# Mixture of experts on one core: three buffers for the groups' mixed rows, group rows turned ahead of the second layer, turned hidden rows apart from their use

## The chip, the cores and the metric

The kernel runs on one NeuronCore of a Trainium2 chip. A core has five engines that run side by side, each through its own instructions in order: TensorE (PE, matrix multiplies; PEld is its weight load), VectorE (DVE), ScalarE (ACT), GpSimd (POOL) and SyncE (SP, which here issues transfers). An instruction starts when the one before it on its engine has started its work and when the semaphores that it waits for have been raised by other engines or by transfers (DMA). The metric is device time in microseconds (us) of one execution; less is better.

## The reference

Two parts follow each other. The first is clustered attention over 4 batches, 8 heads and 768 positions, and its output gives 3072 rows x of 512 numbers. The second is a mixture of 8 experts, and this change is in the second alone:

```python
do_compute = x @ w_skip > 0
xc = x[do_compute]
logits = xc @ w_gate
e_idx = np.argmax(logits, axis=1)
gate_w = softmax(logits)[rows, e_idx]
for e in range(8):
    mask = e_idx == e
    h = np.maximum(xc[mask] @ w1[e], 0.0)      # 512 -> 1024
    y[mask] = gate_w[mask, None] * (h @ w2[e]) # 1024 -> 512
out[do_compute] = xc + y
```

## The kernel before

The attention's last matmuls with its values (L718) end soon after 421 us; the experts' work begins beside that and runs to the end of the kernel. One expert comes first (p = 0), and the others follow in the order of how many rows they have, p = 1 (most) to 7, and the table `SHAPE` says how each is cut: experts 1 and 2 have two tiles of 128 rows, experts 3 to 7 have one, and beside its tiles an expert has groups of 32 rows: expert 2 has group 0, expert 3 has groups 1 and 2, experts 4, 5 and 6 have groups 3, 4 and 5. Rows are fetched by an indirect DMA from GpSimd (`gather`, L1321, tiles `xg` for the 128-row tiles and slices of `PT` for groups) and written back by one (`scatter`, L1328).

**Tiles of 128 rows.** Each product is made of three matmuls of a high and a low half (`three`: L1139, L1140, L1141 in the second layer; L1158, L1161, L1162 in the first layer of a one-tile expert). ScalarE makes the high half of each weight (L1552), VectorE the low half (L1553). Hidden rows are made 512 at a time (`hidden_rows`, and ScalarE's Relu at L1164 into `PT`), and are turned with the rows on the free side by four PE transposes (`turn`, L1149), of which ScalarE copies the high half (L1151) and VectorE makes the low half (L1152). `turn(0)` is for the first four blocks f = 0 to 3 of the second layer, `turn(1)` for f = 4 to 7. `prepare(p + 1)` turns the next expert's rows in the same way (L1149 from `xg`, then L1151 and L1152).

**Groups of 32 rows.** A group's row is spread over four partitions, so that 32 rows fill a tile of 128 by 128. Its way is: `group_turn` (a transpose at L1627 and ScalarE's copy `oxt` at L1629), `group_hidden` (the first layer with plain float32 weights, L1636, and the Relu `ohs` at L1640), `group_back` (two transposes, L1646, and the copy `oht` at L1648) and, when that expert's turn has come, `group_result` (the second layer, L1655; then VectorE's `mix` at L1178 of the product, gate and row into the tile `oyo`, which is scattered). The tile `oyo` has one buffer. For expert p + 1 the first three steps are done in the middle of expert p's second layer, so that they lie beside it.

The order on each engine is set by the order of the code and by a scheduler that moves instructions where their inputs are expected later; semaphores do the rest. Weights come by SyncE's queue into a ring of eight buffers `wraw`, each freed when the matmuls and splits that read it are done.

Of the kernel before, what the change touches and what calls it, by code (L numbers as in the profile page):

```python
# [13 lines left out]
F32 = mybir.dt.float32  # L14
# [9 lines left out]
P = 128  # L24
# [13 lines left out]
E, DM, FF = 8, H * D, 1024  # L38
KD, KF = DM // P, FF // P
# [3 lines left out]
OC = P // OT  # L43
# [50 lines left out]
SHAPE = {1: (2, ()), 2: (2, (0,)), 3: (1, (1, 2)), 4: (1, (3,)), 5: (1, (4,)), 6: (1, (5,)), 7: (1, ())}  # L94


class Kernel:
# [1227 lines left out]
    def scatter(self, rows, ix, apart=True, parts=1):  # L1325

        dst = self.out if parts == 1 else self.out.rearrange("n (c d) -> (n c) d", c=parts)
        put = self.nc.gpsimd.indirect_dma_start(  # L1328
            out=dst, out_offset=bass.IndirectOffsetOnAxis(ap=ix, axis=0), in_=rows, in_offset=None,
            bounds_check=self.ntok * parts - 1, oob_is_err=False)  # L1330
        if apart:
            self.tc.declare_no_dep(put.ins, group="rows", reason="a token is in one slot: rows of two scatters differ")
            self.tc.add_to_no_dep_group("rows", put.ins)
# [190 lines left out]
    def experts(self, ctx):  # L1524
        tc, nc = self.tc, self.nc
        pool = lambda name, bufs, **k: ctx.enter_context(tc.tile_pool(name=name, bufs=bufs, **k))
        xp, hp, ot = pool("xp", 2), pool("hp", 1), pool("ot", 1)
# [6 lines left out]
        def psum(tag, *dims):  # L1534
            q = turns[tag]
            q.rotate(-1)
            t = q[-1][:, :int(np.prod(dims))]
            return t.rearrange("p (a b) -> p a b", a=dims[0]) if len(dims) > 1 else t
# [7 lines left out]
        def split(w, tag, pieces=1, part=slice(None)):  # L1546

            hi, lo = W[f"{tag}h"], W[f"{tag}l"]
            n = 1024 // pieces
            todo = [(slice(c * n, (c + 1) * n), *t) for c in range(pieces) for t in zip(w, hi, lo)]  # L1550
            for cs, r, h, l in todo[part]:
                nc.scalar.activation(out=h[:, cs], in_=r[:, cs], func=AF.Copy)  # L1552
                nc.vector.tensor_tensor(out=l[:, cs], in0=r[:, cs], in1=h.bitcast(F32)[:, cs], op=ALU.subtract)  # L1553
            return hi, lo
# [4 lines left out]
        def prepare(p):  # L1559

            x, n = rows(p), SHAPE[p][0]
            hi, lo = self.X1 if n == 1 else (xp.tile([P, KD, n * P], F32R, name=f"x{n}{c}", bufs=1) for c in "hl")
            self.turned([x[:, j, k * P:(k + 1) * P] for k in range(KD) for j in range(n)], hi, lo, bank)
            return hi, lo
# [60 lines left out]
        def group_turn(x):  # L1625
            tp = psum("tp", P)
            nc.tensor.transpose(out=tp, in_=x, identity=self.ident)  # L1627
            xt = ot.tile([P, KD, OT], F32, name="oxt", bufs=2)
            nc.scalar.activation(out=xt.rearrange("p k t -> p (k t)"), in_=tp, func=AF.Copy)  # L1629
            return xt  # L1630

        def group_hidden(xt, w1):
            ph = psum("ph", FF // OC)
            for k in range(KD):
                for c in range(OC):
                    nc.tensor.matmul(ph[c * OT:(c + 1) * OT, :], lhsT=xt[:, k, :],  # L1636
                                     rhs=w1[k][:, c * FF // OC:(c + 1) * FF // OC],
                                     start=(k == 0), stop=(k == KD - 1), skip_group_check=True)
            hs = ot.tile([P, KF // OC, P], F32, name="ohs", bufs=2)
            nc.scalar.activation(out=hs.rearrange("p m f -> p (m f)"), in_=ph, func=AF.Relu)  # L1640
            return hs

        def group_back(hs):
            th = psum("ph", KF // OC, P)
            for m in range(KF // OC):
                nc.tensor.transpose(out=th[:, m, :], in_=hs[:, m, :], identity=self.ident)  # L1646
            ht = ot.tile([P, KF // OC, OC, OT], F32, name="oht2", bufs=2)
            nc.scalar.activation(out=ht.rearrange("p m c t -> p m (c t)"), in_=th, func=AF.Copy)  # L1648
            return ht

        def group_result(ht, w2, x, oid, og, apart=True):
            py = psum("py", DM // OC)
            for f in range(KF):
                for c in range(OC):
                    nc.tensor.matmul(py[c * OT:(c + 1) * OT, :], lhsT=ht[:, f % (KF // OC), f // (KF // OC), :],  # L1655
                                     rhs=w2[f // 2][:, f % 2 * DM + c * DM // OC:f % 2 * DM + (c + 1) * DM // OC],
                                     start=(f == 0), stop=(f == KF - 1), skip_group_check=True)
            yo = ot.tile([P, DM // OC], F32, name="oyo")
            self.mix(yo, py, x, og)
            scatter(yo, oid, apart, parts=OC)  # L1660

        def rows(p):
            if xg[p % 3] is None:
                xg[0] = xp.tile([P, CT, DM], F32, name="xg0", bufs=1)
            return xg[p % 3]

        def gathers(p):
            for j in range(SHAPE[p][0]):
                gather(rows(p)[:, j, :], self.slots[0][p][:, j:j + 1])
# [5 lines left out]
        def group_first(p):  # L1675

            for g in SHAPE[p][1]:
                backs[g] = group_back(group_hidden(group_turn(self.XG[g]), self.halves[p, 0]))

        def ahead(n):  # L1680
            self.load_pieces(4 * n + RING - 12, 4 * n + RING - 8)


        backs = {}
        gathers(1)
        scatter(self.YE, self.early[0])
        gates = self.slot_gates(self.acc.rearrange("p v h e -> p v (h e)"), ot, P, CT * E, "")
# [2 lines left out]
        py = psum("py", DM)  # L1690
# [7 lines left out]
        xs = prepare(1)  # L1698
# [7 lines left out]
        for p in range(1, E):  # L1706
            tiles, mine = SHAPE[p]
            for g in mine:
                group_result(backs[g], self.halves[p, 1], self.XG[g], *groups[g][1:])
            if tiles == CT:  # L1710
                h = hidden(*xs, *w1s)
            else:
                hidden_rows(0)
                self.turn(0, bank)
                hidden_rows(1)
            if p == 1:
                mark = self.newest()
            w2s = split(self.halves[p, 1], "w2")
            ahead(2 * p + 4)
            if p + 2 < E:  # L1720
                gathers(p + 2)
            if p == 1:
                n0 = self.written()
                self.codes()
                for c in range(OC):
                    nc.vector.memset(self.cblock[c * OT:(c + 1) * OT, :], float(c))
                nc.vector.tensor_copy(self.again.rearrange("p (c t) -> p c t", c=OC),
                                      self.ident[:OT, :OT].unsqueeze(1).to_broadcast([OT, OC, OT]))
                far = ot.tile([P, 1], F32, name="far")
                nc.vector.tensor_scalar(out=far, in0=self.number[:, :1], scalar1=float(self.NG), scalar2=CAP // OT + 1.0,  # L1730
                                        op0=ALU.mult, op1=ALU.add)
                groups = {0: group_lists(group_rows(far))}
                group_gathers(2)
                groups.update(self.group_places(pm, psum, ot))
                group_gathers(3)
                self.hold(n0, mark)
            elif p + 2 < E:
                group_gathers(p + 2)
            if p == 2:
                self.overflow_table(ot)  # L1740
            if p + 1 < E:
                w1s = split(self.halves[p + 1, 0], "w1")
            idx, gate = self.slots[1][p], self.gates[p]
            if tiles == CT:
                for j in range(CT):
                    result(rows(p), *h, *w2s, j, idx[:, j:j + 1], gate[:, j:j + 1])
                    if j == 0:
                        group_first(p + 1)
                        ahead(2 * p + 5)
                        xs = prepare(p + 1)  # L1750
            else:
                py = psum("py", DM)
                for f in range(KF // 2):
                    self.second_layer(py, f)
                if p + 1 < E:
                    group_first(p + 1)
                    ahead(2 * p + 5)
                self.turn(1, bank)
                if p + 1 < E:
                    xs = prepare(p + 1)  # L1760
                for f in range(KF // 2, KF):
                    self.second_layer(py, f)
                finish(py, rows(p)[:, 0, :], idx[:, :1], gate[:, :1])
            if p == E - 2:
                nov = nc.values_load(self.nov[0:1, 0:1], min_val=0, max_val=self.NG)
# [48 lines left out]
```

## Time and profile before

| what | value |
|---|---|
| device time, median of 3 runs | 602.88 us (602.48 to 604.83) |
| the profiled execution's own time | 603.23 us |
| its span in the profile | 601.5 us |
| around the span | 1.73 us |
| PE busy | 582.3 us, 97% of the span |
| chain that ended last | PE 83%, DVE 7%, issue 5%, DMA 2% |
| experts 3 to 7 in that execution | from 509.81 us (PE's first group matmul of expert 3) to 593.2 us |

The profile is one execution, and all times in it are from the span's start. A row of the timeline gives the start, the time taken and the instruction; in brackets, how long its engine had been idle, and what ended that. PE's matmuls are pipelined, so a row's duration overlaps the next row's; what one costs in a row of them is the distance between two starts. The trace counts two records for each float32 matmul of L1636 and L1655.

### The profile page before, as it was taken

Reading aid. Unit: us, or ns where it says so; the run is one execution under the profiler, and the core shown is the slowest. Engines: PE = TensorE matmul, PEld = TensorE weight load, DVE = VectorE, ACT = ScalarE, POOL = GpSimd, SP = SyncE. Lnnn points to the kernel's source line nnn. Section 1 sums busy time; section 2 is a strip of 40 time slices with the busy share of each in tenths; the row PEclk is TensorE's granted clock in tenths of the full one; section 3 lists DMA queues with packets and bytes.
Section 4 is the critical chain, followed back from the end, with each engine's and each line's share of the span. In section 5 each row is a group of like instructions: output and inputs, shape, how many; then the busy total and the mean of one; then the engine's idle time right before and its main releaser. Section 6 shows DMA issues by size and latency. Waiting matters only on the chain.

```text
span 601.5 us, 12901 instructions
## 1 busy us (share of the span) xinstructions
PE 582.3 (97%) x4118; PEld 418.6 (70%) x4118; DVE 488.7 (81%) x1032; ACT 390.5 (65%) x917; POOL 357.9 (59%) x391
## 2 busy tenths in 40 slices
PE   7999999999999999999999999999999999899994
PEld 2566667776677766876776766764689797677773
DVE  7987698798989997999997897888579985566781
ACT  7467768677777866877777775973365444556670
POOL 8966959787868876788776786752203320423210
PEclk9999999999999999999999999999999999999998
DMA  7296685767856776678578666663226674598730
GB/s 221 80 232 146 165 217 148 170 153 176 194 138 177 206 165 154 178 152 204 144 174 197 181 165 151 199 212 117 67 87 218 215 260 159 167 318 286 256 119 17
DMA packets 52517, 105.05 MB, mean 175 GB/s; under 512 B 8395, under 2 KB 22777, under 8 KB 52448
## 3 DMA queue, kind: packets, MB, share of 16 engines
q1 hardware_dynamic: 49904, 97.81, 59.5%
q0 software_dynamic: 2144, 6.19, 2.9%
q8 instruction: 34, 0.56, 0.4%
q14 instruction: 35, 0.29, 0.1%
q10 hardware_dynamic: 400, 0.20, 0.1%
HBM read 55.76 MB, written 9.57 MB: 109 GB/s over the span
## 4 chain that ended last, share of the span: by engine, by line
PE 83%; DVE 7%; issue 5%; DMA 2%; POOL 1%; ACT 1%; SPq 0%; POOLq 0%; ACTq 0%; DVEq 0%
PE ps L718 20%; PE ps L692 12%; PE ps L633 11%; PE ps L693 10%; PE ps L1141 3%; PE ps L1139 3%; PE ps L1140 3%; PE ps L748 2%; PE ps L538 2%; PE ps L1655 2%; PE ps L807 2%; PE ps L1158 2%; PE ps L1636 2%; PE ps L1161 2%; PE ps L1162 1%
## 5 line engine op out<-in xcount | busy, mean ns | idle before, releaser
L635 DVE TENSOR_REDUCE M<-ps 128x1 f32<-128x512 f32 (+1 forms) x374 | 190.8, 550 | 40.1 <-PE ps L633 36.5
L707 POOL TENSOR_TENSOR acc<-acc,PT 128x384 f32<-128x384 f32 x134 | 123.5, 950 | 43.8 <-ACT PT L695 40.6
L692 PE MATMUL ps<-D 98*128 98x384 f32 x384 | 134.9, 351 | 2.4 <-DVE M L635 2.3
L633 PE MATMUL ps<-D 96*128 96x512 f32 (+1 forms) x374 | 129.0, 348 | 2.0 <-ACT D L600 1.9
L707 POOL TENSOR_TENSOR acc<-acc,wraw 128x384 f32<-128x384 f32 x112 | 110.5, 1017 | 33.0 <-ACT wraw L695 27.5
L693 PE MATMUL ps<-D 128*128 128x384 f32 x384 | 130.0, 339 | 0.0
L695 ACT ACTIVATE PT<-ps 128x384 f32<-128x384 f32 x216 | 98.6, 494 | 40.1 <-PE ps L693 31.3
L695 ACT ACTIVATE wraw<-ps 128x384 f32<-128x384 f32 x168 | 77.8, 493 | 16.0 <-PE ps L693 6.5
L692 PEld LDWEIGHTS ps<-D 98*128 98x128 f32 x384 | 72.8, 190 | 19.6 <-issue 6.4
L633 PEld LDWEIGHTS ps<-D 96*128 96x128 f32 x374 | 70.7, 190 | 14.0 <-issue 5.2
L693 PEld LDWEIGHTS ps<-D 128*128 128x128 f32 x384 | 73.1, 190 | 7.5
L718 PE MATMUL ps<-PT,vt 128*64 128x385 f32 x432 | 75.4, 492 | 0.0
L718 PE MATMUL ps<-wraw,vt 128*64 128x385 f32 x336 | 57.9, 492 | 0.0
L718 PEld LDWEIGHTS ps<-PT,vt 128*64 128x64 f32 x432 | 28.8, 136 | 34.8 <-issue 33.9
L1552 ACT ACTIVATE D<-wraw 128x1024 fp32r<-128x1024 f32 (+1 forms) x45 | 44.0, 1005 | 11.2 <-PE ps L1141 9.0
L1328 POOL DMA_INDIRECT out<-yo,ixw x7 | 11.1, 1582 | 57.4 <-DVE yo L1178 51.5
L489 DVE TENSOR_TENSOR raw<-raw,D 128x768 fp32r<-128x768 f32 x28 | 43.5, 1565 | 0.0
L718 PEld LDWEIGHTS ps<-wraw,vt 128*64 128x64 f32 x336 | 22.7, 137 | 27.3 <-issue 26.1
L701 POOL TENSOR_TENSOR acc<-PT 128x384 f32<-128x384 f32 x36 | 30.6, 870 | 14.6 <-ACT PT L695 14.5
L1553 DVE TENSOR_TENSOR D<-wraw,D 128x1024 fp32r<-128x1024 f32 (+1 forms) x29 | 33.9, 1179 | 6.6 <-ACT D L1552 6.4
L829 ACT ACTIVATE x<-ps,rs 128x64 f32<-128x64 f32 x162 | 35.2, 306 | 2.7 <-DVE rs L760 1.2
L701 POOL TENSOR_TENSOR acc<-wraw 128x384 f32<-128x384 f32 x28 | 28.0, 1020 | 5.9 <-ACT wraw L695 5.9
(377 smaller groups left out, 1038.0 us busy)
## 6 DMA issues: line engine op xcount, KB each, us to landing
wraw<-w SPq DMA_DIRECT2D x64, 512.0 KB
D<-D SPq DMA_DIRECT2D x124, 192.0 KB
raw<-qk SPq DMA_DIRECT2D x16, 768.0 KB
D<-raw SPq DMA_DIRECT2D x60, 192.0 KB
vt<-v SPq DMA_DIRECT2D x16, 384.0 KB
out<-x SPq DMA_DIRECT2D x31, 192.0 KB
D<-mk SPq DMA_DIRECT2D x120, 24.0 KB
D<-mr SPq DMA_DIRECT2D x56, 1.5 KB
```

Of the source, the lines that this page charges most:

```text
L489: eng.tensor_tensor(out=lo.bitcast(F32R), in0=lo, in1=c[f"hi{t}"].bitcast(F32), op=ALU.subtract)
L633: nc.tensor.matmul(sm, lhsT=c["qm"][a][0:96, j * P:(j + 1) * P], rhs=c["kb"][a][0:96, m0:m1], start=True, stop=True)
L635: nc.vector.tensor_reduce(out=c["m"][:, j, a, hf:hf + 1], in_=sm, axis=AX.X, op=ALU.max)
L692: nc.tensor.matmul(ps, lhsT=c["kb"][a][0:98, ks], rhs=c["qm"][a][0:98, sl], start=True, stop=False)
L693: nc.tensor.matmul(ps, lhsT=c["kc"][a][:, ks], rhs=c["qc"][a][:, sl], start=False, stop=True)
L695: nc.scalar.activation(out=pt, in_=ps, func=AF.Exp, scale=D ** -0.5)
L701: nc.gpsimd.tensor_tensor(out=acc, in0=self.pt(i, s - 2)[:, :HALF], in1=pt, op=ALU.add)
L707: (nc.vector if dve else nc.gpsimd).tensor_tensor(out=acc, in0=acc, in1=pt, op=ALU.add)
L718: nc.tensor.matmul(av[a * D:(a + 1) * D, :], lhsT=c["vt"][:, kt, a * D:(a + 1) * D], rhs=self.pt(i, hf * 2 * KT + kt * 2 + a), start=(kt = ...
L829: self.nc.scalar.activation(out=c["x"][:, j, cs], in_=xp[:, n, cs], func=AF.Copy, scale=c["rs"][:, j, 2 * hp + a:2 * hp + a + 1])
L1552: nc.scalar.activation(out=h[:, cs], in_=r[:, cs], func=AF.Copy)
L1553: nc.vector.tensor_tensor(out=l[:, cs], in0=r[:, cs], in1=h.bitcast(F32)[:, cs], op=ALU.subtract)
```

## The change

Three edits. The tile `oyo` gets three buffers. For p > 1 the group rows of expert p + 1 are turned (`group_turn`) before the weights of its first layer are split and before expert p's second layer, where they were turned in the middle of it; what is left of the groups' way is cut into `group_first` (L1636, L1640) and `group_middle` (L1646, L1648), with `prepare` and, for one-tile experts, three matmuls of the second layer between them. And `turn(1)` of a one-tile expert is written ahead of its second layer, where it stood in the middle, behind the first half.

```diff
-            yo = ot.tile([P, DM // OC], F32, name="oyo")
+            yo = ot.tile([P, DM // OC], F32, name="oyo", bufs=3)
...
             for g in SHAPE[p][1]:
-                backs[g] = group_back(group_hidden(group_turn(self.XG[g]), self.halves[p, 0]))
+                inner[g] = group_hidden(turned.get(g) or group_turn(self.XG[g]), self.halves[p, 0])
+
+        def group_middle(p):
+
+            for g in SHAPE[p][1]:
+                backs[g] = group_back(inner[g])
...
             if p + 1 < E:
+                if p > 1:
+                    turned.update((g, group_turn(self.XG[g])) for g in SHAPE[p + 1][1])
                 w1s = split(self.halves[p + 1, 0], "w1")
...
                         xs = prepare(p + 1)
+                        group_middle(p + 1)
             else:
                 py = psum("py", DM)
-                for f in range(KF // 2):
-                    self.second_layer(py, f)
-                if p + 1 < E:
-                    group_first(p + 1)
-                    ahead(2 * p + 5)
                 self.turn(1, bank)
-                if p + 1 < E:
-                    xs = prepare(p + 1)
-                for f in range(KF // 2, KF):
+                for f in range(KF):
+                    if p + 1 < E:
+                        if f == KF // 2:
+                            group_first(p + 1)
+                            ahead(2 * p + 5)
+                            xs = prepare(p + 1)
+                        elif f == KF // 2 + 1:
+                            group_middle(p + 1)
                     self.second_layer(py, f)
```

VectorE's instructions keep their order; what moves there is what they wait for. This is VectorE in expert 3, before: the second group matmul result's mix is preceded by the first's, and the waits in brackets name the DMA lanes (`DMASW`) and engines.

```order
L1553 TENSOR_TENSOR D<-wraw,vtW 128x1024 [waits DMAHW2_49,Activation_49]
L1178 SCALAR_TENSOR_TENSOR oyo<-ps,gateg,PT 128x128 [waits DMASW6_49,DMASW2_49,PE_49]
L1178 SCALAR_TENSOR_TENSOR oyo<-ps,gateg,PT 128x128 [waits DMASW3_49,DVE_49,PE_49]
L1553 TENSOR_TENSOR rawW<-wraw,D 128x1024 [waits DMAHW3_49,Activation_49]
L1152 TENSOR_TENSOR D<-ps,D 128x256 [waits Activation_49] x2
```

And the same rows in the changed kernel:

```order
L1553 TENSOR_TENSOR D<-wraw,vtW 128x1024 [waits DMAHW2_49,Activation_49]
L1178 SCALAR_TENSOR_TENSOR oyo<-ps,gateg,PT 128x128 [waits DMASW2_49,PE_49]
L1178 SCALAR_TENSOR_TENSOR oyo<-ps,gateg,PT 128x128 [waits DMASW3_49,PE_49]
L1553 TENSOR_TENSOR rawW<-wraw,D 128x1024 [waits DMAHW3_49,DVE_49,Activation_49]
L1152 TENSOR_TENSOR D<-ps,D 128x256 [waits Activation_49] x2
```

The two mixes now wait for their gathered rows and for PE alone, and no longer for the buffer's earlier reader.

PE in the middle of expert 4's second layer (experts 3 and 5 are alike), before: `PT` into L1627 is the group's rows, `PT` into L1149 the hidden rows of `turn(1)`, and L1636 counts one row for two records of the trace.

```order
L1141 MATMUL ps<-D 128x512
L1627 MATMUL ps<-ident,PT 128x128
L1149 MATMUL ps<-ident,PT 128x128 x4
L1636 MATMUL ps<-wraw,oxt 32x256 x16
L1149 MATMUL ps<-ident,xg_5138 128x128 x4
L1646 MATMUL ps<-ident,ohs 128x128 x2
L1139 MATMUL ps<-D 128x512
```

The same place in the changed kernel; the first row is the first matmul of block f = 2:

```order
L1139 MATMUL ps<-D 128x512
L1149 MATMUL ps<-ident,PT 128x128 x4
L1140 MATMUL ps<-D 128x512
L1141 MATMUL ps<-D 128x512
L1139 MATMUL ps<-D 128x512
L1140 MATMUL ps<-D 128x512
L1141 MATMUL ps<-D 128x512
L1636 MATMUL ps<-wraw,oxt 32x256 x16
L1149 MATMUL ps<-ident,xg_5138 128x128 x4
L1139 MATMUL ps<-D 128x512
L1140 MATMUL ps<-D 128x512
L1141 MATMUL ps<-D 128x512
```

L1627 has gone ahead of the whole second layer, the four turns now have five long matmuls between them and L1636, and the two L1646 stand behind the last row shown. In experts 6 and 7 the four turns have moved up likewise, to behind the first matmul of f = 2 and of f = 1. On ScalarE the copy at L1629 and the copies L1151 of `turn(1)` have each moved ahead of a weight split L1552.

PE in expert 2's second layer, in the difference between the two (`xg_5459` is expert 3's rows):

```order
-L1627 MATMUL ps<-ident,PT 128x128 x2
-L1149 MATMUL ps<-ident,xg_5459 128x128 x2
-L1139 MATMUL ps<-D,hh 128x512
-L1636 MATMUL ps<-wraw,oxt 32x256 x19
-L1646 MATMUL ps<-ident,ohs 128x128 x2
-L1636 MATMUL ps<-wraw,oxt 32x256 x13
-L1149 MATMUL ps<-ident,xg_5459 128x128 x2
+L1636 MATMUL ps<-wraw,oxt 32x256 x32
+L1149 MATMUL ps<-ident,xg_5459 128x128 x4
+L1646 MATMUL ps<-ident,ohs 128x128 x4
```

The two L1627 have gone ahead of the second layer of the first tile, and the groups' matmuls and turns between the two tiles stand in three unbroken blocks. The orders of GpSimd and of SyncE are as before.

## Rows read from the trace of the kernel before

**Rows 1.** The page, part 1: busy time of each engine, share of the span, instructions.

```profile
PE 582.3 (97%) x4118; PEld 418.6 (70%) x4118; DVE 488.7 (81%) x1032; ACT 390.5 (65%) x917; POOL 357.9 (59%) x391
```

**Rows 2.** Waits of PE, 470 to 602 us: total us, times, longest.

```profile
PE ps L1141 <- DVE D L1152: 1.6, 1, 1.6
PE ps L1139 <- ACT D L1151: 0.5, 2, 0.3
PE ps L1655 <- issue: 0.3, 1, 0.3
PE ps L1646 <- ACT ohs L1640: 0.3, 1, 0.3
PE ps L1636 <- ACT D L1552: 0.3, 1, 0.3
PE ps L1636 <- ACT oxt L1629: 0.3, 1, 0.3
```

**Rows 3.** Timeline of DVE: start, duration, instruction, idle time before and its releaser.

```profile
520.00 0.35 DVE L1178 SCALAR_TENSOR_TENSOR oyo<-ps,gateg,PT 128x128 f32<-128x128 f32 x1 [7.06 <-DMA out<-oyo,idwg]
...
521.40 0.75 DVE L1152 TENSOR_TENSOR D<-ps,D 128x256 fp32r<-128x256 f32 x2
...
538.74 0.75 DVE L1152 TENSOR_TENSOR D<-ps,D 128x256 fp32r<-128x256 f32 x2
```

**Rows 4.** Timeline of POOL: a scatter of layer 3, a gather of group rows.

```profile
513.86 0.98 POOL L1328 DMA_INDIRECT out<-oyo,idwg  x1 [0.30 <-issue]
...
525.65 1.01 POOL L1321 DMA_INDIRECT PT<-out,idrg  x1 [0.31 <-issue]
```

**Rows 5.** Timeline of PE: the start of layer 3's second layer.

```profile
519.62 0.39 PE L1139 MATMUL ps<-D 128*128 128x512 f32 x1
...
521.87 0.50 PE L1141 MATMUL ps<-D 128*128 128x512 f32 x1 [1.63 <-DVE D L1152]
```

**Rows 6.** Timeline of PE, layer 4's second layer, to layer 5's first group matmul.

```profile
538.81 0.39 PE L1139 MATMUL ps<-D 128*128 128x512 f32 x1
...
541.72 0.60 PE L1149 MATMUL ps<-ident,PT 128*128 128x128 f32 x4
542.60 1.93 PE L1636 MATMUL ps<-wraw,oxt 128*32 128x256 f32 x32 [0.28 <-ACT D L1552]
544.47 0.66 PE L1149 MATMUL ps<-ident,xg 128*128 128x128 f32 x4
545.11 0.44 PE L1646 MATMUL ps<-ident,ohs 128*128 128x128 f32 x2
545.30 0.47 PE L1139 MATMUL ps<-D 128*128 128x512 f32 x1
...
548.24 0.97 PE L1655 MATMUL ps<-wraw,oht 128*32 128x128 f32 x28
```

**Rows 7.** Timeline of PE: four transposes between long matmuls, layer 4's first layer.

```profile
536.49 0.66 PE L1149 MATMUL ps<-ident,PT 128*128 128x128 f32 x4
536.90 0.48 PE L1161 MATMUL ps<-D 128*128 128x512 f32 x1
537.21 0.40 PE L1162 MATMUL ps<-D 128*128 128x512 f32 x1
```

**Rows 8.** Timeline of ACT: the second Relu of layer 4.

```profile
539.90 0.60 ACT L1164 ACTIVATE PT<-ps 128x512 f32<-128x512 f32 x1
```

**Rows 9.** Timeline of PE: the two groups' matmuls in expert 2.

```profile
499.30 2.36 PE L1636 MATMUL ps<-wraw,oxt 128*32 128x256 f32 x38
...
501.74 0.44 PE L1646 MATMUL ps<-ident,ohs 128*128 128x128 f32 x2
...
503.95 0.44 PE L1149 MATMUL ps<-ident,xg 128*128 128x128 f32 x2
```

**Rows 10.** DMA issues, 440 to 602 us: KB each, median us to landing.

```profile
PT<-out,idrg POOLq DMA_INDIRECT x5, 3.3
```

**Rows 11.** Windows: busy us by engine (instructions), PE clock, DMA share, GB/s.

```profile
558.00:560.00 2.00, 1.72 (x11) 1.24 (x10) 2.00 (x3) 2.00 (x4) 0.53 (x1) 1.00 0.04 16
```

More of the change, by code (lines that the diff above doesn't have):

```diff
@@ L1677, in group_first @@
             for g in SHAPE[p][1]:
-                backs[g] = group_back(group_hidden(group_turn(self.XG[g]), self.halves[p, 0]))
+                inner[g] = group_hidden(turned.get(g) or group_turn(self.XG[g]), self.halves[p, 0])
+        def group_middle(p):
+            for g in SHAPE[p][1]:
+                backs[g] = group_back(inner[g])
         def ahead(n):
             self.load_pieces(4 * n + RING - 12, 4 * n + RING - 8)
-        backs = {}
+        inner, backs, turned = {}, {}, {}
         gathers(1)
```

## The prediction, as it was put on record

> **What bounds the kernel now.** I read the page first: PE is busy for 582.3 of 601.5 us, 97% [rows 1]. So PE's own stream sets the time, nearly from end to end, and a change pays only where PE stands idle, or where it saves or adds PE work. This change saves no PE work: it turns the same rows and multiplies the same tiles. I then read PE's waits from 470 us on, where all that is edited lies [rows 2]. The reader is to see how little is left: one wait of 1.6 us for VectorE's low half (L1152), two of together 0.5 for ScalarE's copies L1151, and three of 0.3 around the groups' matmuls, 3.0 us without the one put down to issue. Each of these has its place in the edits. Last I read the timelines at these places, since PE's ends are modelled and a wait shown as idle is shorter than the time lost between starts.
>
> **The third-buffer edit (expert 3).** VectorE's second mix into `oyo` starts at 520.00 after 7.06 us of waiting for the scatter of the first [rows 3]; that scatter had been issued at 513.86, so it held the buffer for 520.00 - 513.86 = 6.1 us [rows 4]. Behind the mix in VectorE's queue stand a weight split and the two L1152 of `turn(0)`, which so came at 521.40 [rows 3]. PE had started the second layer at 519.62 and needs the first L1152 for its third matmul. It started that at 521.87 [rows 5]; at the spacing of long matmuls, 0.23 us (I read it from twelve of them and their entry: 548.24 - 545.30 = 2.94 = 12 x 0.23 + 0.18 [rows 6]), it would have been at 519.62 + 0.46 = 520.08. Lost: 1.79 us.
>
> What is late next? Expert 4 runs the same code without the buffer wait: there L1152 starts at 538.74, 0.07 before the second layer's first matmul at 538.81 [rows 3, 6]. Put on expert 3 this gives 519.62 - 0.07 = 519.55; the pair takes 0.75, its first half under 0.42, so the low half is there at 519.97, and PE asks for it at 520.08, or later by the turn L1627 that now stands ahead. So I take the whole 1.8. Bounds: 1.8, and nothing if another wait of VectorE's takes its place. Experts 4 to 6 have one group each, a layer apart, and gain nothing from buffers.
>
> By the Trainium skill (DMA: Bandwidth & Descriptors, "Anatomy of one DMA — SWDGE (gpsimd) path") a transfer of this kind takes 2.0 us and its bytes over 436 GB/s, an estimate of 2.2 us for these 64 KB. By it the buffer would be free near 516, before VectorE's next input, and this edit would be worth nothing. The trace's 6.1 us decides against it here.
>
> **The turns set apart (experts 3 to 5).** I cost expert 4 from its second layer's first matmul to the next expert's first group matmul: 548.24 - 538.81 = 9.43 us [rows 6]. In it the four turns of L1149 start at 541.72 and L1636 at 542.60, 0.88 later, where four turns between long matmuls take 536.90 - 536.49 = 0.41 [rows 6, 7]: some 0.45 are lost to the wait shown as 0.28. L1646 comes 0.64 behind the next four turns, where I would allow 0.50. The new order, summed by the same rows: L1627 alone 0.20 (a quarter of 0.41, and 0.09 for stepping back to long matmuls: the first one behind turns takes 537.21 - 536.90 = 0.31 [rows 7] and not 0.23, some 0.09 with rounding); seven long matmuls 1.61; four turns 0.41; the step and five long ones 1.24; L1636 542.60 to 544.47, 1.87; four turns of `xg` 0.50; step and three long 0.78; two L1646 0.19 (545.11 to 545.30); step and nine long 2.16; step to the group matmuls 0.09. Sum 9.05, a gain of 0.38 us.
>
> That holds if no input is late. The turns of `turn(1)` need the second Relu, which starts at 539.90 and takes 0.60 [rows 8]: ready at 540.50. PE comes to them at 538.81 + 0.20 + 1.61 = 540.62. Margin 0.12, thin but there. L1636 needs the copy L1629, now ahead of a weight split, a microsecond earlier than before; L1646 has three long matmuls, 0.78, to cover the Relu L1640. Expert 3 has its 0.3 in front of L1646 and expert 5 its 0.3 in front of L1636 [rows 2]; I take 0.36 for each of the three, 1.1 together. Bounds: nothing, if the margin is gone and a new wait as long comes in, and 0.58 each (1.7), if the steps cost nothing.
>
> **Experts 6 and 7.** They have no group to prepare behind them; the wait is that of the first matmul of f = 4 for ScalarE's copy of turns made just before, two of 0.25 idle [rows 2]. With the 0.17 by which a shown wait falls short of the loss (0.45 against 0.28 in expert 4), 0.42 each. The turns now stand eight and more long matmuls ahead. Less one step of 0.09 each: 0.66, taken as 0.7. Bounds 0 and 0.84.
>
> **Expert 2.** From the first L1636 at 499.30 to the turns at 503.95 are 4.65 us, with two L1646 from 501.74 among them [rows 9]. The matmuls are twice the 1.87 of expert 4, and the pair 0.19, together 3.93: 0.72 lost in being broken up and in waits for the group's Relu. In one block the second L1646 pair still comes close behind its Relu, and a gap put down to PE's own issue, such as the 0.3 of another block [rows 2], need not go. I take 0.3. Bounds 0 and 0.7.
>
> **The sum.** 1.8 + 1.1 + 0.7 + 0.3 = 3.9 us off the profiled execution's 603.23: 599.3. That execution is 0.35 above the median of 602.88, so on the median's scale 599.0, 0.65% faster. All bounds at once: from 0 to 1.8 + 1.7 + 0.84 + 0.7 = 5.0 us, 597.9 to 602.9. What comes behind PE's last matmul, a mix and a scatter, is not touched, and starts as much earlier.
>
> **The rivals.** Only the buffer pays: the moved turns trade the old waits for the copies against steps between short and long matmuls (three more for each of three experts, 9 x 0.09 = 0.8 us, already in my sum) and against the thin margin of 0.12. For it: every saving here is under half a microsecond. Against: the rows above, by which a step costs 0.09 and a wait 0.45. Gain 1.8 to 2.1: 601.0. By the Trainium skill (TensorE: Matmul & The Clock Gate, "The mechanism" under packing) weights load beside running matmuls only if they go to other rows of the array, so that each change of the stationary tile would show; in that page's figure a load of 128 columns is 0.11 us (an estimate from "LDWEIGHTS (loading the stationary operand)"), which for the nine steps gives 1.0 us and not 0.8. This trace has 0.08 to 0.09 for a step.
>
> Only the turns pay: VectorE is held by something else in expert 3, such as ScalarE's weight split in front of the second Relu, and `oyo` was the last of two waits. Against it: expert 4 shows the same queue with no such wait. Gain 2.1: 600.8. The Trainium skill's figure for a transfer, cited above, would lead to this case too.
>
> Nothing to see: the scheduler's order or the loads eat both. The weights' loads have no such share: at 558 to 560, late in expert 5, DMA is at 0.04 of its time [rows 11], so what could be loaded by then has been. Gain under 1: 602.4.
>
> Slower: the group's turn now stands ahead of the second layer, and PE cannot pass it. If the gathered rows were late, every microsecond would be PE's. Expert 5's group is gathered at 525.65 [rows 4], gathers of this sort land in 3.3 us [rows 10], and L1627 comes at 538.81: a margin of 9.9 us. It decides only if the landing takes over 13 us, and to end 0.5% slower PE must stand for 3 + 3.9 = 6.9 us, over the three experts: 606.
>
> **How the numbers follow.** Mine 0.62, with its own range 598.1 to 600.2; only the buffer 0.14; only the turns 0.10; nothing to see 0.09; slower 0.05. The range reaches over the two middle cases and not to the last two: 597.9 to 601.6. Half a per cent, 3.0 us, is about what a measurement of this kernel can tell from no change; faster by that means under 599.87. My own case reaches past that at its upper end: faster 0.59, same 0.37, slower 0.04.
>
> **What would show it.** Right: VectorE's second `oyo` at about 513.8 with no wait on a transfer, PE's third second-layer matmul of expert 3 with no idle time before it, 9.0 to 9.1 us from expert 4's second layer to the next group matmul, and no L1636 or L1139 that waits for ScalarE. Wrong: a wait of the four turns for the Relu L1164 in experts 3 to 6, of the last turns of `xg` for L1152, or of L1627 for a transfer; or a new wait of VectorE's behind `oyo`.

## The result, and the profile after

The changed kernel takes 598.47 us (median of 6 runs, 597.92 to 598.84), the kernel before in the same set 602.83 (6 runs, 602.48 to 604.83). The ratio is 0.9919, with a 95% interval of 0.9904 to 0.9934: 0.8% faster, 4.4 us. The profiled execution after took 597.92 us with a span of 596.2, where the one before took 603.23 with 601.5. Of these 5.31 us, 0.80 lie ahead of the first place where PE's order differs: PE starts expert 2's first layer (its first L1139) at 481.63 after and at 482.43 before, and from 440 us up to there its rows stand in the same order in both. 4.5 us are left to explain.

PE is again the engine that sets the time. Part 1 of the page after answers to [rows 1]:

```profile
PE 578.9 (97%) x4118; PEld 416.6 (70%) x4118; DVE 486.9 (82%) x1032; ACT 390.6 (66%) x917; POOL 358.6 (60%) x391
```

The work is the same, 4118 instructions. In the view of PE's waits from 465 to 600 us (engine, line, releaser, total us, times, longest) nothing is left of [rows 2] but a little issue time, and one short wait of 0.2, that of L1158, is new (L1612 waits ahead of 470 us in both kernels):

```profile
PE ps L1655 <- issue: 0.5, 2, 0.3
PE ps L1612 <- DVE orhs L1606: 0.3, 1, 0.3
PE ps L1158 <- ACT D L1151: 0.2, 1, 0.2
```

The 1.6 us for VectorE's low half and the waits of L1139, L1636 and L1646 for ScalarE are gone. The timeline of VectorE after, at the place of [rows 3]:

```profile
512.78 0.35 DVE L1178 SCALAR_TENSOR_TENSOR oyo<-ps,gateg,PT 128x128 f32<-128x128 f32 x1 [1.48 <-PE ps L1655]
...
517.99 0.75 DVE L1152 TENSOR_TENSOR D<-ps,D 128x256 fp32r<-128x256 f32 x2
```

The second mix into `oyo` now waits for PE's product alone, and no longer for a scatter. So the low half is begun at 517.99, 0.08 us ahead of the second layer of expert 3, which starts at 518.07. The timeline of PE after, in four pieces that answer to [rows 9], [rows 5], [rows 6] and the start of the last expert (start, duration, instruction, idle time and its releaser):

```profile
498.08 3.66 PE L1636 MATMUL ps<-wraw,oxt 128*32 128x256 f32 x64
501.67 0.66 PE L1149 MATMUL ps<-ident,xg 128*128 128x128 f32 x4
502.16 0.60 PE L1646 MATMUL ps<-ident,ohs 128*128 128x128 f32 x4
502.52 0.47 PE L1139 MATMUL ps<-D,hh 128*128 128x512 f32 x1
...
518.07 0.48 PE L1139 MATMUL ps<-D 128*128 128x512 f32 x1
518.38 0.40 PE L1140 MATMUL ps<-D 128*128 128x512 f32 x1
518.61 0.39 PE L1141 MATMUL ps<-D 128*128 128x512 f32 x1
...
534.95 0.27 PE L1627 MATMUL ps<-ident,PT 128*128 128x128 f32 x1
534.97 0.48 PE L1139 MATMUL ps<-D 128*128 128x512 f32 x1
...
536.45 0.40 PE L1139 MATMUL ps<-D 128*128 128x512 f32 x1
536.68 0.63 PE L1149 MATMUL ps<-ident,PT 128*128 128x128 f32 x4
537.07 0.48 PE L1140 MATMUL ps<-D 128*128 128x512 f32 x1
537.38 0.39 PE L1141 MATMUL ps<-D 128*128 128x512 f32 x1
...
538.07 0.40 PE L1141 MATMUL ps<-D 128*128 128x512 f32 x1
538.40 1.93 PE L1636 MATMUL ps<-wraw,oxt 128*32 128x256 f32 x32
540.27 0.66 PE L1149 MATMUL ps<-ident,xg 128*128 128x128 f32 x4
540.68 0.47 PE L1139 MATMUL ps<-D 128*128 128x512 f32 x1
...
541.45 0.38 PE L1646 MATMUL ps<-ident,ohs 128*128 128x128 f32 x2
541.59 0.48 PE L1139 MATMUL ps<-D 128*128 128x512 f32 x1
...
543.84 1.95 PE L1655 MATMUL ps<-wraw,oht 128*32 128x128 f32 x64
...
572.50 0.40 PE L1140 MATMUL ps<-D 128*128 128x512 f32 x1
573.11 0.50 PE L1158 MATMUL ps<-rawW,D 128*128 128x512 f32 x1 [0.21 <-ACT D L1151]
```

Expert 2's group work is three unbroken blocks. In expert 3, L1141 comes 0.54 us after L1139, where it came 2.25 after it. Expert 4's stretch, 9.43 us before, is 543.84 - 534.95 = 8.89 with L1627 in it. And one wait has moved: L1158, the first matmul of expert 7's rows, which stands in expert 6's second layer, comes 0.61 us after its neighbour, where two long matmuls stand 0.23 apart.

I measured each stage in the same way in every kernel, from starts in PE's timeline, so that what lies ahead of the experts drops out: expert 2 from its first layer to expert 3's first group matmul, experts 3, 4 and 5 from one group matmul to the next, expert 6 from there to the second layer of expert 7, and expert 7 from that to its last matmul. These are of one execution of each kernel. In the last two sets single executions of most kernels, the kernel before included, took up to 8 us longer than their median, so differences under 1 us are read from the stages. In us:

| kernel | 2 | 3 | 4 | 5 | 6 | 7 |
|---|---|---|---|---|---|---|
| before | 27.38 | 21.03 | 17.40 | 17.32 | 21.02 | 6.21 |
| changed | 26.55 | 18.77 | 16.89 | 16.85 | 21.00 | 5.76 |
| changed, run once more | 26.54 | 18.81 | 16.87 | 16.89 | 21.02 | 5.75 |
| three buffers alone | 27.38 | 19.22 | 17.32 | 17.31 | 21.00 | 6.23 |
| turns alone, one buffer | 26.54 | 20.52 | 16.92 | 16.86 | 21.02 | 5.75 |
| all, two buffers | 26.54 | 18.75 | 16.86 | 16.85 | 21.02 | 5.72 |
| `turn(1)` alone | 27.39 | 23.23 | 17.44 | 17.42 | 21.01 | 5.76 |
| `turn(1)` and three buffers | 27.40 | 19.30 | 17.42 | 17.40 | 21.00 | 5.75 |
| groups alone, one buffer | 26.54 | 21.21 | 16.99 | 17.08 | 20.34 | 6.24 |
| groups and three buffers | 26.54 | 19.54 | 17.00 | 17.05 | 20.39 | 6.22 |
| expert 7's rows earlier, two buffers | 26.54 | 18.79 | 16.86 | 16.86 | 20.77 | 5.74 |

The gains of the changed kernel are 0.83, 2.26, 0.51, 0.47, 0.02 and 0.45, together 4.54 us, as much as is left of the two profiled executions' difference, 4.51.

### The profile page after: what moved, and what is told of

It reads as the page before. It is cut to its first block, busy times and chain, and to the rows that moved or that the text cites. A ratio compares the mean times of both kernels' runs of the same rounds, so it can differ in the third digit from the quotient of the medians.

```text
span 596.2 us, 12896 instructions
## 1 busy us (share of the span) xinstructions
PE 578.9 (97%) x4118; PEld 416.6 (70%) x4118; DVE 486.9 (82%) x1032; ACT 390.6 (66%) x917; POOL 358.6 (60%) x391
## 4 chain that ended last, share of the span: by engine, by line
PE 84%; DVE 6%; issue 4%; DMA 2%; POOL 1%; ACT 1%; SPq 1%; POOLq 0%; ACTq 0%; DVEq 0%
PE ps L718 21%; PE ps L692 12%; PE ps L633 11%; PE ps L693 11%; PE ps L1139 4%; PE ps L1140 4%; PE ps L1141 4%; PE ps L748 2%; PE ps L538 2%; PE ps L807 2%; PE ps L1158 2%; PE ps L1655 2%; PE ps L1161 2%; PE ps L1162 2%; PE ps L1636 2%
## 5 line engine op out<-in xcount | busy, mean ns | idle before, releaser
L707 POOL TENSOR_TENSOR acc<-acc,wraw 128x384 f32<-128x384 f32 x112 | 112.0, 1031 | 31.4 <-ACT wraw L695 25.9
L1552 ACT ACTIVATE D<-wraw 128x1024 fp32r<-128x1024 f32 (+1 forms) x45 | 43.9, 1009 | 8.8 <-PE ps L1141 7.0
L489 DVE TENSOR_TENSOR raw<-raw,D 128x768 fp32r<-128x768 f32 x28 | 41.7, 1501 | 0.0
```

The costliest lines, as they stand in the source:

```text
L489: eng.tensor_tensor(out=lo.bitcast(F32R), in0=lo, in1=c[f"hi{t}"].bitcast(F32), op=ALU.subtract)
L707: (nc.vector if dve else nc.gpsimd).tensor_tensor(out=acc, in0=acc, in1=pt, op=ALU.add)
```

## The experiments

**The buffer and the turns apart.** The first kernel is that of before with the one line of the buffer:

```diff
-            yo = ot.tile([P, DM // OC], F32, name="oyo")
+            yo = ot.tile([P, DM // OC], F32, name="oyo", bufs=3)
```

> The kernel before with three buffers for oyo and nothing else. My theory (two mechanisms that add up): 1.8 us off the median of before, 602.8 to 601.0; PE's wait for L1152 at the start of expert 3's second layer (1.6 us idle) is gone, VectorE's second oyo of expert 3 waits for no transfer, and PE's short waits around L1636, L1646 and L1139 stay (1.4 us idle in all). Rival A, only the buffer pays: 4.4 us off, 598.5, the time of the changed kernel. Rival B, only the turns pay: no change, 602.8, with another wait of VectorE's in front of the same L1152.

Measured: 599.77 us beside 601.19, ratio 0.9976 (0.9967 to 0.9986). PE's waits from 465 to 600 us in this kernel:

```profile
PE ps L1636 <- ACT oxt L1629: 0.9, 3, 0.3
PE ps L1139 <- ACT D L1151: 0.5, 2, 0.3
```

The wait for L1152 is gone and short ones of 1.4 us stand. Expert 3 gains 1.81 us and no other stage more than 0.1. Why the scatter held the one buffer so long was not tested. What the windows of the kernel before show is that the DMA engines' share was 0.93 to 1.04 from 514 to 520 us, while the scatter was under way, and 0.39 from 520 on, where VectorE's second mix starts (stretch, its length, then busy time of PE, PEld, DVE, ACT and POOL with instructions, PE's granted clock, DMA share, GB/s):

```profile
518.00:520.00 2.00, 2.00 (x10) 1.50 (x8) 0.00 (x1) 2.00 (x5) 0.00 (x0) 1.00 1.04 398
520.00:522.00 2.00, 0.37 (x3) 0.14 (x2) 2.00 (x4) 2.00 (x3) 1.38 (x1) 1.00 0.39 146
```

The second kernel is the changed one with one buffer (the line above taken back).

> The changed kernel with oyo back at one buffer. My theory: 4.4 - 1.8 = 2.6 us off the kernel before, 600.2; the short waits of PE are gone, and its wait for L1152 in expert 3 stands as before, 1.6 us idle. Rival A, only the buffer pays: 602.8. Rival B, only the turns pay: 598.5, with no wait of PE in expert 3.

Measured: 599.32 us beside 601.19, ratio 0.9965 (0.9952 to 0.9979). Its waits are the mirror image:

```profile
PE ps L1141 <- DVE D L1152: 1.5, 1, 1.5
PE ps L1158 <- ACT D L1151: 0.2, 1, 0.2
```

The gains stand in experts 2 to 5 and 7, 2.75 us together. Each part carries a share, and "only the buffer" and "only the turns" both fall. By the medians the parts give 1.4 and 1.9 us, together 3.3 where the kernel with both (the next one) gives 4.1 in the same set; by the stages they add up, 1.90 and 2.75 beside 4.54.

**How many buffers.** The changed kernel with `bufs=2`:

> The changed kernel with two buffers for oyo where it has three. My theory: as the changed kernel, 598.5, since only expert 3 has two groups in one layer, and expert 2's scatter lies 20 us and more before. If the third buffer carries something of its own (a scatter that is still under way a layer later): a wait on a transfer comes back in front of an oyo, up to 1.8 us, 600.3.

Measured: 597.12 us beside 601.19, ratio 0.9934 (0.9920 to 0.9948), with the stages of the changed kernel to 0.04 us. The third buffer carries nothing: expert 3 has two groups, and no expert more.

**Each half of the turns.** Here `turn(1)` alone goes ahead of the second layer, and the groups stay in its middle, with one buffer:

```diff
                 py = psum("py", DM)
+                self.turn(1, bank)
                 for f in range(KF // 2):
                     self.second_layer(py, f)
                 if p + 1 < E:
                     group_first(p + 1)
                     ahead(2 * p + 5)
-                self.turn(1, bank)
-                if p + 1 < E:
                     xs = prepare(p + 1)
```

> The kernel before with turn(1) written ahead of the second layer in one-tile experts and nothing else: the groups' way stays in one piece in the middle, oyo keeps one buffer. My theory: the waits of L1139 for ScalarE's copies go in experts 6 and 7 (0.4 us in expert 7; in expert 6 it only moves to L1158), and in experts 3 to 5 some 0.2 us each, since the turns no longer stand in front of L1636, but L1646 still follows its Relu closely: 1.0 us off the median of before. Rival, the parting of turns from long matmuls costs what it saves: no change, with 0.3 us or more between the steps in each expert. PE's 1.6 us for L1152 in expert 3 stays in both.

Measured: 604.55 us (12 runs, 601.09 to 609.31) beside 602.06, ratio 1.0042 (1.0007 to 1.0077): slower by 0.4%, the interval just clear of 1. Theory and rival both failed: neither forecast a loss. In the profiled execution (604.86 us) expert 7 gains its 0.45, but expert 3 loses 2.20. The timeline of PE in this kernel, at expert 3's second layer:

```profile
518.35 0.40 PE L1139 MATMUL ps<-D 128*128 128x512 f32 x1
518.58 0.40 PE L1140 MATMUL ps<-D 128*128 128x512 f32 x1
521.53 0.50 PE L1141 MATMUL ps<-D 128*128 128x512 f32 x1 [2.56 <-DVE D L1152]
521.87 0.57 PE L1139 MATMUL ps<-D 128*128 128x512 f32 x1
522.24 0.63 PE L1140 MATMUL ps<-D 128*128 128x512 f32 x1
522.67 0.63 PE L1141 MATMUL ps<-D 128*128 128x512 f32 x1
```

PE's stand, the stretch in which it starts nothing, is longer: 521.53 - 518.58 = 2.95 us between starts, where it was 2.02 in the kernel before. And behind it the matmuls come 0.43 us apart and not 0.23. The windows of this kernel say why:

```profile
520.00:522.00 2.00, 0.47 (x2) 0.43 (x3) 2.00 (x5) 1.00 (x2) 1.70 (x1) 0.98 0.01 5
522.00:523.00 1.00, 1.00 (x4) 0.81 (x3) 1.00 (x2) 0.00 (x0) 0.00 (x0) 0.50 0.05 13
...
524.00:525.00 1.00, 1.00 (x5) 0.90 (x4) 1.00 (x2) 0.77 (x3) 1.00 (x1) 0.50 0.00 0
525.00:526.00 1.00, 1.00 (x6) 0.72 (x5) 0.91 (x4) 0.94 (x1) 0.69 (x2) 0.83 0.36 74
```

The granted clock fell to 0.50, from 2.4 to 1.2 GHz, when PE had stood, and came back only within 525 to 526; in the kernel before it stays at 1.00 through the shorter stand (its window 520 to 522, above). Of the 2.20 us lost, 0.93 are the longer stand, and the other 1.27 go with the slower matmuls behind it. This is one execution. The fastest of the twelve, 601.09, is 0.5 us above the fastest of the kernel before in that set, 600.58, so a loss of this size need not come in each. The stand is longer because the scatter of the first `oyo` held the buffer for 519.66 - 512.57 = 7.1 us (VectorE's second mix less the scatter's issue), where [rows 3, 4] give 6.1.

To tell the turn's own price from that of the buffer's wait, the same kernel with three buffers:

> The kernel before with the turn of the slot's rows (turn(1)) ahead of the second layer and with three buffers for oyo. With the turn alone, expert 3's second layer took 13.40 us to the next group matmul against 11.22 before: PE stood 2.6 us for the low half L1152, still held back by the buffer of oyo, and its granted clock stood at 0.50 from 522 to 525. Theory one: the turn itself costs nothing, the longer stand lowers the clock, and with the buffer's wait gone the loss goes with it: expert 3's stretch 9.4 us as with the buffer alone, no granted clock under 0.9 in it, ratio 0.996 to 0.998. Rival: the turn at this place costs by itself (its bank, or VectorE's order): the stretch stays over 10.5 us with the buffer free, and the ratio is 0.999 or more.

Measured: 600.37 us (12 runs, 599.94 to 606.36) beside 602.55, ratio 0.9973 (0.9938 to 1.0009). Expert 3 takes 19.30 us, 3.93 less, and the window of the same place in this kernel has PE at full clock with no time to stand:

```profile
520.00:522.00 2.00, 2.00 (x12) 1.43 (x10) 2.00 (x3) 2.00 (x5) 1.87 (x1) 1.00 0.00 0
```

So the turn itself costs expert 3 next to nothing (19.30 against 19.22 with the buffer alone), and in the two executions profiled the loss hung on the buffer. The time alone does not decide, since its interval reaches over 1 and over theory and rival alike. By the stages, against the kernel with three buffers alone, `turn(1)` is worth little: it gives 0.48 in expert 7 and takes 0.08 to 0.10 in each of experts 3 to 5, 0.19 in all. There L1636 still waits for the copy L1629 of L1627, which stands only two long matmuls ahead of it (0.6 us in three waits). Whether the earlier turn made the scatter's 7.1 us or the execution did is open: one profile shows it, and other kernels with one buffer (turns alone 6.2, groups alone 6.1) don't.

The other half: groups turned early and set apart, `turn(1)` left in the middle, first with one buffer and then with three (the edit is against the changed kernel).

```diff
                 py = psum("py", DM)
-                self.turn(1, bank)
-                for f in range(KF):
-                    if p + 1 < E:
-                        if f == KF // 2:
-                            group_first(p + 1)
-                            ahead(2 * p + 5)
-                            xs = prepare(p + 1)
-                        elif f == KF // 2 + 1:
-                            group_middle(p + 1)
+                for f in range(KF // 2):
+                    self.second_layer(py, f)
+                if p + 1 < E:
+                    group_first(p + 1)
+                    ahead(2 * p + 5)
+                self.turn(1, bank)
+                if p + 1 < E:
+                    xs = prepare(p + 1)
+                for f in range(KF // 2, KF):
+                    if p + 1 < E and f == KF // 2 + 1:
+                        group_middle(p + 1)
```

> The changed kernel with oyo at one buffer and turn(1) back in the middle of the second layer: only the group rows' turn ahead, and group_middle apart from group_first. My theory: expert 2 gives its 0.84 us as in the changed kernel (26.5 us from its first L1139 to the group matmuls of expert 3, 27.4 before), experts 3 to 5 some 0.2 to 0.3 us each, experts 6 and 7 nothing: 1.5 us off the median of before. Rival: the gain of expert 2 comes from turn(1) as well, or the rest of the moves is worth nothing without it: under 0.8 us off.

Measured: 599.84 us beside 602.06, ratio 0.9975 (0.9949 to 1.0002), 2.2 us off the median with an interval that reaches 1; the stages give 1.96 us. Expert 2 gives its whole 0.84 here, and the waits of L1139 for L1151 stay (0.5 us in two). The columns of experts 3 and 6 are not to be read by themselves in the two kernels with the groups alone: in the second layers of experts 3, 4 and 5 now stand three first-layer matmuls of the next expert, as here in the kernel with three buffers:

```profile
523.96 0.47 PE L1158 MATMUL ps<-rawW,D 128*128 128x512 f32 x1
524.27 0.39 PE L1161 MATMUL ps<-D 128*128 128x512 f32 x1
524.50 0.39 PE L1158 MATMUL ps<-rawW,D 128*128 128x512 f32 x1
```

That puts 3 x 0.23 = 0.69 us more into expert 3's stretch and takes as much out of expert 6's. With this put back the groups alone, with one buffer, gain 0.51, 0.41 and 0.24 in experts 3 to 5, and nothing in experts 6 and 7.

> The changed kernel with turn(1) put back into the middle of the second layer: groups set apart and three buffers, without the slot's turn ahead. If the turn of the slot's rows adds to the groups' share (theory one), this lies 0.5 to 1.0 us above the changed kernel, since the waits of L1139 for ScalarE's copies L1151 (0.5 us in two) come back: ratio to before 0.993 to 0.995. If only the groups' share counts (rival), it equals the changed kernel within 0.3 us.

Measured: 598.39 us beside 602.55, ratio 0.9935 (0.9904 to 0.9965), and 0.69 above the changed kernel run beside it (below); the two intervals lie on each other, so the times alone do not show it. By the stages `turn(1)` does add to the groups' share, 0.92 us: with the 0.69 put back, 0.1 in experts 3, 4 and 6 each, 0.2 in expert 5 and 0.46 in expert 7. That is far more than the 0.19 that it gives without the groups' moves, so the two halves of the turns help each other and are not a sum.

**The rival that would have made it slower.** Two kernels fetch the group rows of expert p + 1 only in expert p, one expert later than they do, the first with the rest as before, the second with the change:

```diff
-            elif p + 2 < E:
-                group_gathers(p + 2)
+            elif 2 < p < E - 1:
+                group_gathers(p + 1)
```

> The kernel before, but the group rows of experts 4, 5 and 6 are gathered one expert later than they were: behind the same scatters and gathers of the expert in whose second layer they are turned. My theory (PE cannot pass a turn whose rows are late): issued at about 525.7, 544 and 561 and landing 3.3 us later, against turns at 524.3, 541.6 and 559.0, PE waits at L1627 some 5 us three times, 15 us more than before. Rival, the gathers have room to spare or the landing hides behind the matmuls: under 3 us more.

> The changed kernel with the same late gathers. My theory: the turn now comes 2.7 us earlier, ahead of the second layer, so each of three waits is 2 to 3 us longer than in the kernel before with late gathers: some 8 us three times, 24 us over the changed kernel. So the changed order would be the slower one of the two if gathers were late. Rival, the order of the turn does not matter: the same loss in both, within 2 us.

Measured, both beside 602.06: 620.90 us (ratio 1.0311, 1.0273 to 1.0349) and 623.71 (1.0359, 1.0321 to 1.0397). The theories hold in kind: 18.8 us lost where 15 were expected, and the changed order is the slower one. PE's longest wait of each, of the first and of the second kernel:

```profile
PE ps L1627 <- DMA PT<-out,idrg: 14.0, 3, 5.1
```

```profile
PE ps L1627 <- DMA PT<-out,idrg: 20.0, 3, 6.8
```

With late rows the changed order stands 6.0 us longer in its three places, 2.0 each on average, since L1627 has been moved ahead of work that could have covered the wait. It loses its own 4.4 us and 2.8 more. Here too the clock falls while PE stands, as a window of the second kernel shows at one of the places, where PE stands from 545.03 to 552.06:

```profile
548.00:552.00 4.00, 0.00 (x0) 0.00 (x0) 0.00 (x0) 0.00 (x0) 2.01 (x2) 0.50 0.28 82
```

**The wait that moved.** L1158 of expert 7 waits for the copy L1151 of turns made only two long matmuls ahead of it. The turns stand at 572.05, but ScalarE has a weight split to do before the copy, as its timeline in the changed kernel shows:

```profile
571.70 1.09 ACT L1552 ACTIVATE D<-wraw 128x1024 fp32r<-128x1024 f32 x1
572.64 0.41 ACT L1151 ACTIVATE D<-ps 128x256 fp32r<-128x256 f32 x1
```

Here expert 7's rows, which have no group behind them, are prepared at the third block of expert 6's second layer instead of the fifth:

```diff
-                        if f == KF // 2:
+                        if f == (KF // 2 if SHAPE[p + 1][1] else 2):
```

> The changed kernel, but in expert 6, which has no group behind it, the next expert's rows are turned at block f = 2 and not at f = 4. My theory of what is left: in the changed kernel's profile expert 6 gave back nothing (7.26 us from its second layer to the next L1161, 7.30 before), because L1158 of expert 7 now waits for ScalarE's copy of rows turned 1 us ahead (0.21 idle, 0.38 between starts); turned earlier this wait goes, and four turns wait up to 0.2 for the Relu L1164: 0.2 to 0.4 us less than the changed kernel, 598.2. Rival: the wait only moves, to the Relu or to the bank that VectorE still reads: 598.5.

Measured: 596.78 us beside 601.19, ratio 0.9932 (0.9918 to 0.9945); expert 6 takes 20.77 us, not 21.00, and the wait is gone. To compare it directly, it ran once more with two buffers, in one set with the changed kernel itself (both beside 602.55):

> The changed kernel with two buffers for oyo and with expert 6's and 7's rows (no group behind them) prepared at the third of the eight steps in the second layer, not the fifth. Theory: the wait of L1158 for the copy L1151 (0.2 us shown, 0.38 lost) goes, 0.2 to 0.4 us under the changed kernel beside it. Rival: what the turns gain there is lost in steps among the long matmuls: equal to it within 0.1 us.

> The changed kernel once more, beside the three others on one chip, so that they can be compared directly: ratio to before 0.990 to 0.994; the wait of L1158 for L1151 shows again at the start of expert 6's successor, 0.2 us.

Measured: 597.14 us (12 runs, 596.41 to 603.33; ratio 0.9928, 0.9893 to 0.9962) and 597.70 (11 runs, 596.87 to 602.94; ratio 0.9926, 0.9893 to 0.9959). Medians and lowest times are 0.6 and 0.5 us under the changed kernel, the stage of expert 6 says 0.25 (21.02 and 20.77); the two intervals lie on each other. In the first set the gap to the two-buffer kernel was 0.3. So it points the right way each time, and no time taken here proves it; the profile shows the wait gone, and shows it again (0.2 us) in the changed kernel run once more.

## Why the prediction was right

599.0 us was predicted and 598.47 measured, inside the likeliest case's own range. Term by term:

- **What bounds it**: right. Every gain is idle time of PE taken away, or a step between short and long matmuls; the work is unchanged.
- **The third buffer, 1.8 us**: right, 1.81 alone and 20.52 - 18.77 = 1.75 on top of the turns. The low half is begun 0.08 ahead of the second layer, predicted 0.07. The count in the edit is one too many: two buffers do it. By the Trainium skill (DMA: Bandwidth & Descriptors, "Anatomy of one DMA — SWDGE (gpsimd) path") the buffer would have come free after an estimated 2.2 us and the edit been worth nothing; the three-buffer kernel decides for the 6.1 us of the trace.
- **The turns of experts 3 to 5, 1.1 us**: the mechanism right, the size too small: 0.45, 0.51 and 0.47, together 1.43. Expert 4 was summed at 9.05 and took 8.89. L1627 costs 0.12 and not 0.20, the turns of `xg` 0.41 and not 0.50, L1646 0.14 and not 0.19; against it stands the step into L1636, 0.33 from the last long matmul, which I had left out (0.09). The rule "0.09 for every step between short and long", on top of the turns' own time, was too dear where few short ones slip between long ones, as L1627 does: 0.02 between starts, and the next long matmul is 0.09 late. So the 9.0 to 9.1 us that were named as a sign came out at 8.89. The thin margin of the four turns was real: the second Relu of expert 4 ends at 536.60 (536.00 and 0.60), the turns start at 536.68, so 0.08 where 0.12 was predicted.
- **Experts 6 and 7, 0.7 us**: 0.02 and 0.45. The step that failed is the like treatment of the two. In expert 6 the removed wait of L1139 came back as one of L1158, 573.11 - 572.50 = 0.61 for 0.23, since the first two turns of `xg` still stood two long matmuls ahead of their use, and ScalarE's split ahead of their copy. I had asked what covers the turns of `turn(1)` and not what covers those of `prepare(7)`. Preparing earlier gets 0.25 us back.
- **Expert 2, 0.3 us**: 0.83, over the bound of 0.7 that I gave. Two steps failed. I took off more than half for waits that I thought would stay, but between the group's matmuls and L1646 now stand four turns of `xg`, 0.49, which cover the Relu. And the bound was made from a stretch without the pieces on its sides (L1627, a pair of `xg` turns, the second pair of L1646), each of which had steps of its own; the one block of L1636 also takes 3.59, less than twice 1.87. From the long matmul ahead of these pieces to the long one behind them, before had 6.51 us with three long matmuls in it: 5.82 without. After, the same pieces take 4.76, and about 0.2 for the two L1627 elsewhere.

The three errors, +0.3, -0.2 and +0.5, leave 4.5 us where 3.9 were summed. That the forecast lands within 0.6 us is in part luck: one term was too large by what another was too small, and the term of expert 2 was less than half of what was there.

**The rivals.** Only the buffer and only the turns each fell by the run with the other part, and "nothing to see" by the 4.4 us. The slower one, PE held at L1627 by late rows, didn't come: no wait of L1627 in the profile after. But its mechanism is there, and the two late kernels gave its price. That its place decides needed a landing over 13 us by the prediction's margin of 9.9; rows fetched an expert later were enough.

What the prediction didn't see is that the buffer's wait had a second price in store: a little longer, and the clock falls with it. The edits were argued as a sum of independent terms, and by the stages the buffer and the turns are. Inside the turns they are not: `turn(1)` is worth 0.19 us beside three buffers and 0.92 with the groups moved as well, and with neither it lost 1.9 in the execution profiled.

## What to carry to other kernels

Where an engine in order is busy for 97% of the span, count the starts on both sides of each wait and each change of shape, over the whole stretch in which pieces are moved: what a bracket shows as idle was less than what was lost, 0.28 for 0.45 and 0.21 for 0.38 at short waits, 1.63 for 1.79 at the long one. When a wait is taken away, ask of every instruction behind it, and not only of those that are moved, how many long ones now cover its input, and what stands ahead of that input on the engine that makes it. And look for a buffer whose reader is a scatter: here a second `oyo` of one tile was worth 1.8 us, and the third nothing.

## What was not expected of the hardware

PE's clock made one stand of 2.95 us dearer than its length: the granted clock fell from 1.00 to 0.50 and stayed there from 522 to some point in 525 to 526, which went with 1.27 us more; in the kernel before, a stand of 2.02 us at the same place left it at 1.00. In the kernels with late rows it fell in each of the six stands, which were 4.4 to 7.2 us, and in the second of these kernels the long matmuls behind them came 0.43 us apart. That PE's clock has a lower level, 1.2 GHz, that follows on idleness, stands in the Trainium skill (TensorE: Matmul & The Clock Gate, "What's actually happening"), and these traces agree. So a short wait in a busy stretch can cost its length alone, and a little longer one more; the two stands of 2.02 and 2.95 us are one execution each.

A 128 by 128 turn between long matmuls cost the same alone and in company. From the long matmul ahead to the second one behind, less two spacings of 0.23, one took 0.12 us (L1627, 534.71 to 535.29) and four took 0.47 (537.38 - 536.45 = 0.93).
